# Moving the logit group, the Q/K stage and the small norm operations in a two-layer transformer kernel

## The chip, the cores and the metric

The kernel runs on one core of one Trainium2 chip. Its time is the device time of one execution in microseconds (us), as a median over executions. Two kernels are compared by a ratio: the mean time of one kernel's fast runs over the mean of the other's fast runs of the same rounds. It is therefore not quite the ratio of the medians that are quoted.

Engine names in the profile: PE is TensorE (matmul), PEld its weight load, DVE VectorE, ACT ScalarE, POOL GpSimd, and SPq the queue of the sync engine (SyncE), which issues nearly all DMAs of this program in program order.

## The reference

Two pairs of layers, with the same weights in both pairs. S = 2048 tokens, D = 1024, F = 3584, 32 heads of 32 channels, bf16.

```python
x = A_x
for _ in range(2):                                   # written out in the original
    x = x + _A_ref(_layernorm(x), A_wqkv, A_wo)      # attention over 8 keys, at distances 0, 2, ..., 14
    x = x + _B_ref(_layernorm(x), B_W_gate, B_W_up, B_W_down)
return x

# _A_ref: qkv = x @ wqkv; logits[s, w] = q[s] . k[s - 2w] * Dh**-0.5; softmax over w;
#         o[s] = sum_w attn[s, w] * v[s - 2w]; return o @ wo
# _B_ref: gate = x @ W_gate; h = relu(gate) * (x @ W_up); return h @ W_down
```

## The kernel before

The work is cut into 8 blocks of 512 tokens (blocks 0 to 3 are the first pair of layers, 4 to 7 the second). A loop runs over the blocks n. One pass does four things on TensorE:

1. the gated unit of block n: 28 pairs of gate and up groups, 448 matmuls of 128x512;
2. the output projection of the attention of block n+1 (64 matmuls), after which the second norm of block n+1 can begin;
3. Q/K of block n+2 (128 matmuls) and, from block 4 on, V (64 matmuls);
4. the down projection of block n, in two halves of 112 matmuls. Each half reads four weight slabs of up to 1 MB, `wd_0_0` to `wd_0_3` and `wd_1_0` to `wd_1_3`.

Meanwhile VectorE forms the products q·k for 8 offsets and sums them over the channel groups; one small matmul group `L` (the logit group, eight matmuls) reduces them over the channels; then come the softmax and the weighting of V on VectorE. The normed block goes to the next matmuls through a transposing DMA of 1 MB (called the copy below). A scheduler orders the instructions of each engine from the order in which they are emitted, the waits, and its own estimate of durations. It also orders the DMAs of SyncE.

The weight slabs come through a ring of five buffers, loaded by SyncE. Cuts are marked `...`.

```python
wring = ctx.enter_context(tc.tile_pool(name="wring", bufs=5))
...
def load_slab(src_ap, name):
    ...
    nc.sync.dma_start(tv, src_ap)
...
def ln_steps(n, which, early=False):       # which: "a" = norm ahead of attention, "b" = ahead of the gated unit
    ...
    def small():                           # once for the four tiles of a block
        st = hold["st"]
        ...
        nc.vector.tensor_scalar(mean[:], st[:, 0, :], 1.0 / D, None, op0=ALU.mult)
        nc.vector.tensor_tensor(nvar[:], st[:, 0, :], mean[:], op=ALU.mult)
        nc.vector.tensor_tensor(nvar[:], nvar[:], st[:, 1, :], op=ALU.subtract)
        nc.vector.tensor_scalar(vpe[:], nvar[:], -1.0 / D, EPS, op0=ALU.mult, op1=ALU.add)
        nc.gpsimd.tensor_tensor(rstd[:], vpe[:], neg_half[:], op=ALU.pow)
        nc.vector.scalar_tensor_tensor(nb[:], mean[:], -1.0, rstd[:], op0=ALU.mult, op1=ALU.mult)
        ...
    def apply(t):
        def f():
            ...
            nc.scalar.activation(hold["xn"][:, t, :], xt[:], ACT.Identity, scale=hold["rstd"][:, t:t + 1],
                                 bias=hold["nb"][:, t:t + 1])
            if t == TPB - 1:
                ...
                nc.sync.dma_start_transpose(hold["xnT"][:].rearrange("p t k n -> p (t k) n"),
                                            hold["xn"][:].rearrange("p t d -> p (t d)"))
        return f
...
    for n in range(NN):
        gu, hold = gu_steps(n, ln_b[n])
        spread(ev, gu, at, 2 * GRP)                      # ev: (time, step) pairs, emitted in order of time
        ...
        if n + 1 < NN:
            spread(ev, wo_steps(n + 1), at, 2 * GRP)     # output projection
            ln2(n + 1, at + 4.5)                         # second norm and its copy
            at += 2 * GRP * TPB
        if n + 2 < NN:
            spread(ev, qk_steps(n + 2, ln_a[n + 2]), at, 2 * GRP)
            sums, red = prod_sum_steps(n + 2)
            spread(ev, sums, at + 3.6, 4.4)
            ev.append((at + 75.5, red))                  # logit group
            ev.append((at + 76.0, lambda n=n: softmax(n + 2)))
            ...
        down = down_steps(n, hold)
        spread(ev, down, at, 4 * GRP)
```

## Time and profile before

The median was 1696.95 us over 3 runs (1695.44 to 1698.25). The profiled execution has a span of 1696.5 us and a mean granted TensorE clock of 0.988 of full speed.

| What | us |
|---|---|
| span | 1696.5 |
| PE busy | 1637.1 (97%) |
| 8 matmuls of 128x512, start to start, undisturbed | 1.727 |
| first gated unit waits for its transposed norm | 11.8 |
| logit groups of blocks 2 to 7 wait for the last sum | 2.9 to 4.9 each, 23.1 in all |

TensorE bounds the kernel, so what counts is where TensorE stands still. This is the line of busy times on the page of the kernel before (busy us, share of the span, instructions):

```profile
PE 1637.1 (97%) x7576; PEld 781.0 (46%) x7576; DVE 1064.2 (63%) x973; ACT 482.8 (28%) x777; POOL 172.5 (10%) x168
```

These are PE's waits in the kernel before. A line gives the tile and line of code that waited, what released it, the sum in us, the number of waits, and the longest.

```profile
PE acc_g L448 <- DMA xnT_b_1286<-xn_b_1168: 11.8, 1, 11.8
...
PE L_2670 L298 <- DVE s_2235 L340: 4.9, 1, 4.9
PE L_9605 L298 <- DVE s_9153 L340: 4.1, 1, 4.1
PE L_6767 L298 <- DVE s_6315 L340: 3.8, 1, 3.8
PE L_4001 L298 <- DVE s_3566 L340: 3.8, 1, 3.8
PE L_5349 L298 <- DVE s_4897 L340: 3.6, 1, 3.6
PE L_8184 L298 <- DVE s_7732 L340: 2.9, 1, 2.9
```

`acc_g` is the first gate group; the `L_` lines are the six logit groups. Most of these holes cost more than their length, as the timeline of PE in the kernel before shows around the first of them (start, length, engine, line, operation, out<-in, count, and in brackets the idle time and its releaser):

```profile
359.36 0.61 PE L298 MATMUL L_2670<-s_2235,sel 128*32 128x512 bf16 x4 [4.89 <-DVE s_2235 L340]
359.90 1.03 PE L474 MATMUL dacc_2550<-wd_1_3_2690,hT_1339 128*128 128x512 bf16 x2
360.73 1.69 PE L474 MATMUL dacc_2551<-wd_1_3_2690,hT_1339 128*128 128x512 bf16 x4
```

Two matmuls, from 359.90 to 360.73, take 0.83 us, that is 0.42 us each, where 0.216 is the undisturbed pace. The Trainium skill ("TensorE: Matmul & The Clock Gate", Part 1: The HAM clock gate) explains such a pace: after an idle window of about 3.4 us the array runs at half clock until it has been busy for about as long.

### The profile page before, as it was taken

Reading aid. Unit: us, or ns where it says so; the run is one execution under the profiler, and the core shown is the slowest. Engines: PE = TensorE matmul, PEld = TensorE weight load, DVE = VectorE, ACT = ScalarE, POOL = GpSimd, SP = SyncE. Lnnn points to the kernel's source line nnn. Section 1 sums busy time; section 2 is a strip of 40 time slices with the busy share of each in tenths; the row PEclk is TensorE's granted clock in tenths of the full one; section 3 lists DMA queues with packets and bytes.
Section 4 is the critical chain, followed back from the end, with each engine's and each line's share of the span. In section 5 each row is a group of like instructions: output and inputs, shape, how many; then the busy total and the mean of one; then the engine's idle time right before and its main releaser. Section 6 shows DMA issues by size and latency. Waiting matters only on the chain.

```text
span 1696.5 us, 18303 instructions
## 1 busy us (share of the span) xinstructions
PE 1637.1 (97%) x7576; PEld 781.0 (46%) x7576; DVE 1064.2 (63%) x973; ACT 482.8 (28%) x777; POOL 172.5 (10%) x168
## 2 busy tenths in 40 slices
PE   7997999989999999999999999999999999999999
PEld 3543445534454444534455344554445434444444
DVE  2699794997279943998149971499615995121111
ACT  7834414023240324222142221422215101130110
POOL 1210002300050001200013000230004100000000
PEclk9998999999999999999999999999999999999999
DMA  8576758546755384766547666476854946465442
GB/s 288 88 193 146 192 172 210 184 139 185 222 143 181 125 224 149 192 158 200 173 158 209 158 186 189 146 203 169 229 171 125 244 156 198 149 191 181 149 152 72
DMA packets 370692, 296.78 MB, mean 175 GB/s; under 512 B 142257, under 2 KB 351153, under 8 KB 369585
## 3 DMA queue, kind: packets, MB, share of 16 engines
q1 hardware_dynamic: 370320, 295.10, 61.0%
q8 instruction: 59, 0.97, 0.2%
q10 hardware_dynamic: 288, 0.52, 0.1%
q14 instruction: 25, 0.20, 0.0%
HBM read 256.77 MB, written 21.00 MB: 164 GB/s over the span
## 4 chain that ended last, share of the span: by engine, by line
PE 64%; DVE 25%; ACT 4%; DMA 3%; issue 2%; POOL 2%; DVEq 0%; SPq 0%; POOLq 0%; ACTq 0%
PE acc_g L448 23%; PE acc_u L448 23%; PE acc_wo L423 7%; DVE ac_0_2236 L340 1%; DVE ac_1_5145 L340 1%; DVE ac_1_3813 L340 1%; DVE ac_1_2482 L340 1%; DVE ac_1_9401 L340 1%; DVE ac_1_7980 L340 1%; DVE ac_1_6563 L340 1%; PE acc_q L273 1%; PE acc_k L273 1%; POOL rstd L165 1%; PE acc_v L242 1%; DVE ac_0_3567 L340 1%
## 5 line engine op out<-in xcount | busy, mean ns | idle before, releaser
L453 ACT ACTIVATE r<-acc_g 128x512 bf16<-128x512 f32 x224 | 133.2, 595 | 637.2 <-PE acc_g L448 628.5
L165 POOL TENSOR_TENSOR rstd<-vpe,neg_half 128x4 f32<-128x4 f32 x17 | 22.5, 1326 | 1181.5 <-DVE vpe L163 1181.5
L357 ACT ACTIVATE d<-d 128x1024 f32<-128x1024 f32 x8 | 8.5, 1057 | 258.3 <-DVE d L356 258.3
L454 DVE TENSOR_TENSOR hT_10755<-acc_u,r 128x512 bf16<-128x512 f32 x28 | 19.4, 692 | 77.4 <-PE acc_u L448 77.4
L454 DVE TENSOR_TENSOR hT_9720<-acc_u,r 128x512 bf16<-128x512 f32 x28 | 19.4, 692 | 53.0 <-PE acc_u L448 53.0
L454 DVE TENSOR_TENSOR hT_6878<-acc_u,r 128x512 bf16<-128x512 f32 x28 | 19.3, 691 | 52.8 <-PE acc_u L448 52.8
L454 DVE TENSOR_TENSOR hT_5461<-acc_u,r 128x512 bf16<-128x512 f32 x28 | 19.3, 690 | 52.5 <-PE acc_u L448 52.5
L454 DVE TENSOR_TENSOR hT_8299<-acc_u,r 128x512 bf16<-128x512 f32 x28 | 19.3, 691 | 51.2 <-PE acc_u L448 51.2
L454 DVE TENSOR_TENSOR hT_4043<-acc_u,r 128x512 bf16<-128x512 f32 x28 | 19.3, 690 | 39.7 <-PE acc_u L448 39.7
L454 DVE TENSOR_TENSOR hT_2712<-acc_u,r 128x512 bf16<-128x512 f32 x28 | 19.3, 688 | 38.9 <-PE acc_u L448 38.9
L474 PEld LDWEIGHTS <-hT_4043 128*128 128x128 bf16 x224 | 22.5, 101 | 28.6 <-issue 3.9
L474 PEld LDWEIGHTS <-hT_5461 128*128 128x128 bf16 x224 | 22.5, 101 | 28.5 <-issue 3.7
L474 PEld LDWEIGHTS <-hT_2712 128*128 128x128 bf16 x224 | 22.4, 100 | 28.5 <-issue 3.7
L474 PEld LDWEIGHTS <-hT_8299 128*128 128x128 bf16 x224 | 22.2, 99 | 27.7 <-issue 2.4
L474 PEld LDWEIGHTS <-hT_1339 128*128 128x128 bf16 x224 | 22.0, 99 | 27.4 <-issue 2.0
L474 PEld LDWEIGHTS <-hT_10755 128*128 128x128 bf16 x224 | 21.9, 98 | 26.4
L474 PEld LDWEIGHTS <-hT_9720 128*128 128x128 bf16 x224 | 21.9, 98 | 26.4
L474 PEld LDWEIGHTS <-hT_6878 128*128 128x128 bf16 x224 | 21.8, 98 | 26.4 <-issue 0.2
L454 DVE TENSOR_TENSOR hT_1339<-acc_u,r 128x512 bf16<-128x512 f32 x28 | 19.3, 690 | 19.7 <-PE acc_u L448 16.3
L448 PE MATMUL acc_g<-xnT_b_1286,wg_0_1340 128*128 128x512 bf16 x32 | 9.2, 441 | 11.8 <-DMA xnT_b_1286<-xn_b_1168 11.8
L359 DVE TENSOR_REDUCE ssum<-d 128x128 f32<-128x1024 f32 x8 | 15.4, 1924 | 5.6 <-ACT d L357 5.6
L298 PEld LDWEIGHTS <-sel 128*32 128x32 bf16 x120 | 2.9, 95 | 34.4 <-issue 34.0
(1893 smaller groups left out, 3872.3 us busy)
## 6 DMA issues: line engine op xcount, KB each, us to landing
vhm_372<-v_d SPq DMA_DIRECT2D x4, 284.0 KB, 5.7
vhm_1298<-v_d SPq DMA_DIRECT2D x4, 284.0 KB, 8.9
vhm_2480<-v_d SPq DMA_DIRECT2D x4, 284.0 KB, 6.1
vhm_3811<-v_d SPq DMA_DIRECT2D x4, 284.0 KB, 9.1
vhm_5235<-v_d SPq DMA_DIRECT2D x4, 284.0 KB, 6.6
vhm_6653<-v_d SPq DMA_DIRECT2D x4, 284.0 KB, 6.4
vhm_8070<-v_d SPq DMA_DIRECT2D x4, 284.0 KB, 7.2
vhm_9491<-v_d SPq DMA_DIRECT2D x4, 284.0 KB, 6.0
```

Source lines behind the costliest of these rows:

```text
L165: nc.gpsimd.tensor_tensor(rstd[:], vpe[:], neg_half[:], op=ALU.pow)
L242: nc.tensor.matmul(acc[:], lhsT=sl[g][:, kc, col:col + P], rhs=ln["xnT"][:, :, kc, :], start=(kc == 0), stop=(kc == KC - 1))
L273: nc.tensor.matmul(acc[:], lhsT=w, rhs=ln["xnT"][:, :, kc, :], start=(kc == 0), stop=(kc == KC - 1))
L298: nc.tensor.matmul(st["L"][32 * tq:32 * tq + 32, WH * wh:WH * (wh + 1), :], lhsT=sel[:], rhs=prod[:, WH * wh:WH * (wh + 1), tq * P:(tq + 1 ...
L340: nc.vector.tensor_tensor(o, ac[:], t[:], op=ALU.add)
L357: nc.scalar.activation(d[:], d[:], ACT.Exp, scale=scale)
L359: nc.vector.tensor_reduce(ssum[:], d[:].rearrange("p w t -> p t w"), axis=AX.X, op=ALU.add)
L423: nc.tensor.matmul(acc[:], lhsT=st["oT"][:, c, t, :], rhs=sl[half][:, c, :], start=(c == 0), stop=(c == KC - 1))
L448: nc.tensor.matmul(acc[:], lhsT=hold[nm][:, kc, jl * P:(jl + 1) * P], rhs=ln["xnT"][:, :, kc, :], start=(kc == 0), stop=(kc == KC - 1))
L453: nc.scalar.activation(r[:], acc[:], ACT.Relu)
L454: nc.vector.tensor_tensor(hold["hT"][:, j, :], accs["u"][:], r[:], op=ALU.mult)
L474: nc.tensor.matmul(ac[t], lhsT=hT[:, j, t * P:(t + 1) * P], rhs=wsl[:, jl, :], start=(j == 0), stop=(j == FC - 1))
```

## The change

Its intent was to take out the holes listed above:

1. The logit group of block n+2 and its softmax go out of the down projection into the next gated unit, behind the first pair of gate and up groups.
2. Q/K (and V) of block n+2 go ahead of the output projection of block n+1, so that VectorE's products and sums begin earlier. The two halves of the projection are run one after the other, and the Q and K groups get a new order among themselves.
3. The order of TensorE's groups is fixed by explicit edges, so that the scheduler cannot move them. One more edge puts each load of V (`vhm`) behind the slab load that was emitted last, and the opening ahead of the loop is timed anew; the cut below doesn't show these.
4. The small norm operations leave VectorE's queue: five ScalarE operations of 128x1 per tile, and one GpSimd power per tile in place of one per block. The second norm of block 0 is transposed tile by tile.

The core of the diff:

```diff
+    @contextmanager
+    def pe_group():
+        if tail_pe[0] is None:
+            yield
+        else:
+            with tc.issue_after(tail_pe[0]):
+                yield
...
-        def small():
-            st = hold["st"]
...                                        # the batch on VectorE shown above
+                nc.scalar.activation(nm2, sx, ACT.Square, scale=1.0 / D)
+                nc.scalar.activation(nm2, nm2, ACT.Identity, scale=-1.0, bias=eps_col[:])
+                nc.scalar.activation(vpe, sq, ACT.Identity, scale=1.0 / D, bias=nm2)
+                nc.gpsimd.tensor_tensor(rstd, vpe, neg_half[:, 0:1], op=ALU.pow)
+                nc.scalar.activation(mr, sx, ACT.Copy, scale=-1.0 / D)
+                nc.scalar.activation(nb, mr, ACT.Identity, scale=rstd)
...
+                if which == "b" and n == 0:
+                    nc.sync.dma_start_transpose(hold["xnT"][:, t, :, :], xn)
+                elif t == TPB - 1:
                     nc.sync.dma_start_transpose(hold["xnT"][:].rearrange("p t k n -> p (t k) n"),
                                                 hold["xn"][:].rearrange("p t d -> p (t d)"))
...
+        elif n + 1 < NN:
+            ev.append((at + 0.1, reds_n[n + 1]))
+            ev.append((at + 0.2, lambda n=n: softmax(n + 1)))
...
-        if n + 1 < NN:
-            spread(ev, wo_steps(n + 1), at, 2 * GRP)
-            ln2(n + 1, at + 4.5)
-            at += 2 * GRP * TPB
         if n + 2 < NN:
-            spread(ev, qk_steps(n + 2, ln_a[n + 2]), at, 2 * GRP)
+            spread(ev, qk_steps(n + 2, ln_a[n + 2]), at, GRP)
             sums, red = prod_sum_steps(n + 2)
-            spread(ev, sums, at + 3.6, 4.4)
-            ev.append((at + 75.5, red))
-            ev.append((at + 76.0, lambda n=n: softmax(n + 2)))
+            reds_n[n + 2] = red
+            spread(ev, sums, at + GRP * (K_STEP[0] + 1.0), 4.4)
...
+        if n + 1 < NN:
+            spread(ev, wo_steps(n + 1), at, 2 * GRP)
+            ln2(n + 1, [at + GRP * TPB + GRP * (t + 1) + 0.1 for t in range(TPB)])
+            at += 2 * GRP * TPB
```

## The prediction

> **What bounds it now.** TensorE. The page shows PE 97% busy; in the timeline 8 matmuls of 128x512 start every 1.727 us, so the 7424 of them cost 1603 us. With 15.2 us before, 15 logit groups of 0.55 and 4.3 us after, the floor is about 1631 us. The span is 1696.5: some 60 us are holes in TensorE's stream.
>
> **The holes (PE's waits and timeline).**
> - Logit groups of blocks 2 to 7 stand inside the down projection and wait for the last DVE sum: 4.9, 3.8, 3.6, 3.8, 2.9, 4.1 us. Afterwards matmuls start every 0.42 us for 2 to 4 us; together about 34 us.
> - First gated unit: 11.8 us for the transposed norm of block 0, plus 1.6 us of slow clock. Its chain: small norm operations on DVE queued behind 2.3 us sums (145.4 to 155.8), applies 4.6 us, one 1 MB transpose 6.8 us.
> - First output projection: 2.1 us for its DMA, 1.7 us slow.
> - Q/K of block 0: 3 to 4 us of waits for products; ACT is busy 35 of 40 us there.
> - K weights: 0.3 to 1.6 us per block, 3 us in all.
>
> The Trainium skill ("TensorE: Matmul & The Clock Gate", Part 1) says an idle window of about 3.4 us drops the array to half clock; this trace agrees (0.42 us per matmul after the 11.8 us hole).
>
> **What the change does.** No matmul is added or removed. The logit group goes behind the first gate/up pair of the next gated unit; Q/K moves ahead of the output projection. The sums take 67.6 us of DVE (30 operations of 2.26 us). They now have Q/K (27.6) + V (13.8) + output projection (13.8) + down (48.4) + 3.5 us, less 8 us until the first K: 99 us, without V (blocks 2, 3) 85. DVE needs 76 to 78 with its evictions of 0.64 us. So all six waits should go. The first gated unit's norm leaves the DVE queue and is transposed per tile: its input should come about when V of block 3 ends, so the 12 us go. Cost: five 128x1 ACT operations per norm tile, estimated 0.1-0.2 us each (the 128x1 accumulator read lasts 0.19), 5-10 us in the opening, where ACT is full; and ACT now waits in order for POOL's power (1.0 to 3.0 us). So the opening gains little, and the first projection still waits for its DMA.
>
> **Sum.** 1697 - 33 (logit groups) - 14 (first gated unit) - 3 (K weights) = 1647 us. All of it lies on the critical path (TensorE).
>
> **Predicted: 1647 us, range 1637 to 1664.** Faster by over 2%: 0.90; within 2%: 0.09; slower: 0.01.
>
> **What would show it.** Logit groups of blocks 2-7 waiting under 0.5 us, sums ending some 10 us before them; granted clock near 1.00 from the first gated unit on, which starts at 152-157 us instead of 167; first projection still waiting 2-4 us; ACT over 85% busy from 30 to 70 us.
>
> **What would make it wrong.** The down projection's second half needs banks whose evictions now stand behind the sums in DVE's order (from block 4 on, with under 2 us of slack by my estimate): holes of 1-3 us per block, with slow clock after them. ACT delaying Q/K in the opening by 5 us or more. POOL, slowed by DVE, holding ACT and the gate evictions. The second K weight slab landing late.

## More of the kernel before

One more view matters, and the prediction did not weigh it: the timeline of SyncE's queue in the kernel before, where block 1 is normed (start us, length of the issue, queue, line, kind of DMA, out<-in).

```profile
291.56 4.91 SPq L177 DMA_TRANSPOSE xnT_b_2241<-xn_b_2117  x1
...
305.28 0.40 SPq L134 DMA_DIRECT2D wd_0_1_2446<-in_B_W_down_dram  x1
...
307.87 1.06 SPq L134 DMA_DIRECT2D wd_1_0_2553<-in_B_W_down_dram  x1
```

The copy of block 1's second norm is issued at 291.56, some 16 us ahead of the slab `wd_1_0`. The output projection's matmuls end at 280.0, so the norm takes about 11.5 us from there to the copy.

## The result, and the profile after

The kernel after took 1721.7 us (median of 4 runs, 1720.78 to 1723.74); the kernel before took 1696.24 (median of 4 in the same comparison). The ratio is 1.015 (95% interval 1.0132 to 1.0168): the change made the kernel 1.5% slower. The predicted time, 1647, and its whole range lie below what was measured. The profiled span is 1719.2 us at a mean granted clock of 0.978.

The busy line of the page of the kernel after, with columns as before:

```profile
PE 1637.0 (95%) x7576; PEld 781.2 (45%) x7576; DVE 1047.8 (61%) x888; ACT 534.5 (31%) x1117; POOL 273.7 (16%) x220
```

TensorE has the same work to the last instruction, in a longer span: the loss is idle time. These are PE's waits in the kernel after:

```profile
PE dacc_2642 L104 <- DMA wd_1_0_2646<-in_B_W_down_dram: 12.2, 1, 12.2
PE dacc_3999 L104 <- DMA wd_1_0_4003<-in_B_W_down_dram: 12.2, 1, 12.2
...
PE dacc_9780 L104 <- DMA wd_1_0_9784<-in_B_W_down_dram: 8.1, 1, 8.1
PE dacc_5446 L104 <- DMA wd_1_0_5450<-in_B_W_down_dram: 8.0, 1, 8.0
PE dacc_6890 L104 <- DMA wd_1_0_6894<-in_B_W_down_dram: 7.9, 1, 7.9
PE dacc_8333 L104 <- DMA wd_1_0_8337<-in_B_W_down_dram: 7.8, 1, 7.8
PE acc_g L104 <- DMA xnT_b_1207<-xn_b_1206: 5.1, 1, 5.1
```

The six logit groups are gone from the list, as intended. In their place stand six waits for the slab `wd_1_0`, one in each down projection of blocks 0 to 5: 56.2 us in all. The list says "DMA". It does not say why the DMA came late. The timeline of SyncE's queue in the kernel after says it, in the pass that corresponds to the one shown before:

```profile
294.23 0.37 SPq L151 DMA_DIRECT2D wd_0_3_2613<-in_B_W_down_dram  x1
294.64 1.86 SPq L399 DMA_DIRECT2D vhm_2567<-v_d  x1
326.87 4.90 SPq L186 DMA_TRANSPOSE xnT_b_2429<-xn_b_2428  x1
331.87 0.52 SPq L151 DMA_DIRECT2D wd_1_0_2646<-in_B_W_down_dram  x1
```

Nothing is issued for 30 us, from 296.5 to 326.87. Then comes the copy, and only behind it the slab, although nothing in the slab's load depends on the copy. The queue is in order, and it stood waiting for the norm. The table of busy times in that stretch shows the DMA engines were not the limit (the window, then us, busy time and count of PE, PEld, DVE, ACT and POOL, granted clock, DMA share, GB/s):

```profile
290.00:331.90 41.90, 35.28 (x164) 15.79 (x162) 41.76 (x29) 16.85 (x40) 17.38 (x6) 0.95 0.46 92
```

The DMA engines were busy 46% of it and moved 92 GB/s, against 173 on average over this span. VectorE, on the other hand, was busy throughout: 41.76 of 41.90 us.

What it costs is in the timeline of PE in the kernel after:

```profile
324.25 1.03 PE L104 MATMUL dacc_2482<-wd_0_3_2613,hT_1392 128*128 128x512 bf16 x4
337.51 3.60 PE L104 MATMUL dacc_2642<-wd_1_0_2646,hT_1392 128*128 128x512 bf16 x8 [12.23 <-DMA wd_1_0_2646<-in_B_W_down_dram]
340.89 2.03 PE L104 MATMUL dacc_2643<-wd_1_0_2646,hT_1392 128*128 128x512 bf16 x8
...
367.03 0.61 PE L104 MATMUL L_2801<-s_2208,sel 128*32 128x512 bf16 x8
```

The first 8 matmuls behind the hole take 3.38 us, 0.42 each: half pace again, 1.65 us lost beyond the 12.2. In the hole that goes with the norm of block 3 (8.0 us, in the down projection of block 2) it is 1.66 us in the first 8 and 0.51 in the next 8. An estimate for six holes: 56.2 us and some 2 us each, 68 us. The last line above answers to the first of the `L_2670` lines before: the logit group starts with no wait.

Why was the norm so late? The projection's matmuls end at 300.9, and the copy is issued 26 us later (11.5 before). Two parts make it up. First, the projection's evictions now stand in VectorE's order among products and sums of 2.3 us each, because Q/K comes first: the last eviction ends at 307.0, 6.0 us behind the matmuls (0.9 before). Secondly, from there to the copy it takes 19.9 us (10.6 before), and GpSimd shows most of the reason. The timeline of POOL in the kernel after, the four powers of block 1's second norm:

```profile
301.97 2.01 POOL L173 TENSOR_TENSOR st_b_2427<-st_b_2427,neg_half 128x1 f32<-128x1 f32 x1 [10.74 <-ACT st_b_2427 L172]
309.19 7.00 POOL L173 TENSOR_TENSOR st_b_2427<-st_b_2427,neg_half 128x1 f32<-128x1 f32 x1 [5.21 <-ACT st_b_2427 L172]
...
318.12 2.60 POOL L173 TENSOR_TENSOR st_b_2427<-st_b_2427,neg_half 128x1 f32<-128x1 f32 x1
322.62 2.62 POOL L173 TENSOR_TENSOR st_b_2427<-st_b_2427,neg_half 128x1 f32<-128x1 f32 x1 [1.91 <-ACT st_b_2427 L172]
```

The same line of code, taken over the whole program, gives the duration with VectorE at rest, in block 7 (op, count, ns min/median/max, first and last start), and who waited for it (us, times):

```profile
L173 POOL TENSOR_TENSOR st_b_10661<-st_b_10661,neg_half x4: 548/550/551, 1522.9 to 1532.4; 128x1 f32<-128x1 f32 x4
...
  ACT st_b_2427 L175: 11.3, 4
```

A power of 128x1 takes 0.55 us at rest and 2.0 to 7.0 us next to the products and sums. The Trainium skill ("GPSIMD Engine Reference", Specifications) states that GpSimd shares its SBUF interfaces with VectorE and contends with VectorE instructions that have two SBUF inputs. The products and sums are such instructions, and this trace agrees. ScalarE, in order, waited 11.3 us for these four powers.

### The profile page after: what moved, and what is told of

Read it like the earlier page. It is cut to its first block, busy times and chain, and to the rows that moved or that the text cites. A ratio compares the mean times of both kernels' runs of the same rounds, so it can differ in the third digit from the quotient of the medians.

```text
span 1719.2 us, 18662 instructions
## 1 busy us (share of the span) xinstructions
PE 1637.0 (95%) x7576; PEld 781.2 (45%) x7576; DVE 1047.8 (61%) x888; ACT 534.5 (31%) x1117; POOL 273.7 (16%) x220
## 4 chain that ended last, share of the span: by engine, by line
PE 65%; DVE 11%; ACT 5%; POOL 4%; issue 3%; DMA 2%; SPq 2%; DVEq 0%; ACTq 0%; POOLq 0%
PE acc_g L104 23%; PE acc_u L104 22%; PE acc_q L104 3%; SPq L186 2%; PE acc_k L104 1%; POOL st_b_3784 L173 1%; PE acc_wo L104 1%; DVE ac_0_7810 L363 1%; DVE ac_0_9257 L363 1%; DVE ac_0_6367 L363 1%; POOL st_b_5235 L173 0%; POOL st_b_6679 L173 0%; POOL st_b_8122 L173 0%; PE dacc_5446 L104 0%; PE dacc_6890 L104 0%
## 5 line engine op out<-in xcount | busy, mean ns | idle before, releaser
L104 PEld LDWEIGHTS <-hT_7019 128*128 128x128 bf16 x224 | 22.5, 101 | 36.4 <-DMA wd_1_0_8337<-in_B_W_down_dram 8.3
L104 PEld LDWEIGHTS <-hT_5575 128*128 128x128 bf16 x224 | 22.5, 101 | 36.3 <-DMA wd_1_0_6894<-in_B_W_down_dram 8.3
L173 POOL TENSOR_TENSOR st_b_10661<-st_b_10661,neg_half 128x1 f32<-128x1 f32 x4 | 2.2, 550 | 159.2 <-ACT st_b_10661 L172 159.2
L173 POOL TENSOR_TENSOR st_a_8704<-st_a_8704,neg_half 128x1 f32<-128x1 f32 x4 | 6.7, 1680 | 73.3 <-ACT st_a_8704 L172 73.3
L173 POOL TENSOR_TENSOR st_a_5814<-st_a_5814,neg_half 128x1 f32<-128x1 f32 x4 | 6.7, 1682 | 73.2 <-ACT st_a_5814 L172 73.2
L173 POOL TENSOR_TENSOR st_a_7257<-st_a_7257,neg_half 128x1 f32<-128x1 f32 x4 | 6.7, 1680 | 73.2 <-ACT st_a_7257 L172 73.2
```

The source lines that it names most:

```text
L104: tail_pe[0] = nc.tensor.matmul(*args, **kwargs).ins
L173: nc.gpsimd.tensor_tensor(rstd, vpe, neg_half[:, 0:1], op=ALU.pow)
```

## The experiments

Theory (call it the queue theory): the whole loss comes from the place of the copy in SyncE's queue, ahead of `wd_1_0`, together with a norm that is late. Rivals: the lateness of the norm by itself; GpSimd's slow powers; the order of Q/K and projection; the edges; the norm operations on ScalarE. The edge on the V loads has no run of its own, but e1, e2 and e10 keep it and have no slab wait. In each of the short diffs below the kernel is compared with the kernel after, unless said otherwise.

The results in one table. The ratio is to the kernel before in the same rounds; "slab waits" is the sum of TensorE's waits for `wd` in the profiled run.

| Run | median us | ratio (95%) | slab waits us |
|---|---|---|---|
| e1, copy behind `wd_1_2` | 1650.79 | 0.9731 (0.9715 to 0.9748) | none |
| e2, copy from ScalarE's queue | 1651.67 | 0.9734 (0.9719 to 0.9748) | none |
| e3, no GpSimd power (wrong result) | 1668.14 | 0.9832 (0.9818 to 0.9847) | 13.7 |
| e4, before + logit group moved | 1662.09 | 0.9795 (0.9781 to 0.981) | none |
| e5, projection first again | 1678.93 | 0.9892 (0.9877 to 0.9907) | none |
| e6, one power per block | 1697.14 | 1.0006 (0.9987 to 1.0024) | 31.1 |
| e7, e1 + e6 | 1652.85 | 0.9739 (0.9725 to 0.9754) | none |
| e8, no edges on TensorE | 1721.34 | 1.0144 (1.0129 to 1.0159) | 56.4 |
| e10, small norm operations back on VectorE | 1653.67 | 0.9744 (0.973 to 0.9757) | none |
| e11, e10 + copy ahead of the slab | 1727.99 | 1.0182 (1.0168 to 1.0196) | 63.0 |
| e9, e1 + sums held back in the opening | 1648.04 | 0.971 (0.9697 to 0.9723) | none |

The medians of the kernel before lay between 1696.89 and 1697.34 us in the three sets of runs (e1 to e4; e5 to e8; e9 to e11). All results but that of e3 were correct.

### e1: the copy of the second norm behind the third slab of the down projection's second half

```diff
-                elif t == TPB - 1:
-                    nc.sync.dma_start_transpose(...)
+                elif t == TPB - 1 and which == "a":
+                    xpose()
...
+        def xpose_late():
+            with tc.issue_after(tail_sp[0]):       # behind the last slab load emitted so far: wd_1_2
+                xpose()
...
         spread(ev, down, at, 4 * GRP)
+        if n + 1 < NN:
+            ev.append((at + 4 * GRP * 6 + 0.5, ln_b[n + 1]["late"]))
```

> The changed kernel with one edit: the transposed copy of the second norm (blocks 1 to 7) is issued behind the down projection's slab loads instead of ahead of four of them. Theory Q (the copy, whose input is ready only at 326.9 us in block 1, stands at the head of SyncE's DMA queue and holds the slab that TensorE needs): the six holes of 12.2, 12.2, 8.0, 7.9, 7.8, 8.1 us and the slow clock after them (about 2.5 us each) go, about 71 us, so 1645 to 1660 us, with the copy landing some 10 us before the next gated unit. Theory N (the second norm is simply too late for what follows): the holes move to the first gate matmuls of the next gated unit, over 5 us each, and the time stays above 1690. Theory F (the fixed TensorE order forbids other work from filling in): no change, 1715 to 1725, since the order stays.

Measured: 1650.79 us. The norm is as late as ever: this is SyncE's queue in e1, where `wd` stands for any of the down slabs.

```profile
315.24 0.37 SPq L151 DMA_DIRECT2D wd<-in_B_W_down_dram  x1
327.16 4.87 SPq L190 DMA_TRANSPOSE xnT_b<-xn_b  x1
332.13 0.53 SPq L151 DMA_DIRECT2D wd<-in_B_W_down_dram  x1
```

The copy is issued at 327.16 (326.87 in the kernel after), but three slabs of the second half are already on their way. The edge was meant to put the copy behind all of them; the last one, `wd_1_3`, still comes behind it, in every block. TensorE needs that slab last (in the kernel after its matmuls start 22.5 us behind those of `wd_1_0`), and no slab wait is left. The next gate group starts at 349.58 without a wait. The span falls from 1719.2 to 1649.0 us, 70.2 us, beside the estimate of 68 above, and the granted clock rises to 0.999. A late norm costs nothing here; a late norm ahead of a load that TensorE needs at once does.

### e2: the copy issued from ScalarE's queue

```diff
-                    nc.sync.dma_start_transpose(...)
+                    (nc.scalar if which == "b" else nc.sync).dma_start_transpose(...)
```

> The changed kernel with the same copy at the same place in the program, but issued from ScalarE's DMA queue (all second norms), so that SyncE's queue holds no wait for the norm. Theory Q: 1645 to 1660 us, no wait for the down slabs above 1 us, although the norm itself is as late as before (copy issued at about 325 to 330 us in block 1). Theory N: as above, waits at the next gated unit, over 1690. Theory F: no change. A cost of about 5 us of ScalarE per block for issuing may show, off the critical path.

Measured: 1651.67 us, no slab waits. The edit moves the copies of blocks 1 to 7; block 0's, tile by tile, stay on SyncE's queue. The timeline of ACT in e2 shows the copy behind the last apply, as late as before, and again without harm:

```profile
326.78 1.24 ACT L182 ACTIVATE xn_b<-x,st_b 128x1024 bf16<-128x1024 bf16 x1
328.05 5.95 ACTq L186 DMA_TRANSPOSE xnT_b<-xn_b  x1
```

This says the same as e1 with a different edit: it is SyncE's queue that was held. The Trainium skill ("DMA: Bandwidth & Descriptors", Anatomy of one DMA — SWDGE (gpsimd) path) states that a DMA's semaphore wait happens on the issuing sequencer before dispatch. That section is written for DMAs issued by GpSimd; the timelines agree for SyncE, which in the kernel after issued nothing for 30 us. The same page (Silent corruption: two transposing streams in flight at once) warns that transposes issued from two engines may not overlap in time. In e2 the two kinds of copy lie in different stages, and its result was correct; e1 does not raise the question.

### e3: no power on GpSimd in the second norms of blocks 1 to 7 (wrong result)

```diff
-                nc.gpsimd.tensor_tensor(rstd, vpe, neg_half[:, 0:1], op=ALU.pow)
+                if which == "b" and n > 0:
+                    nc.scalar.activation(rstd, vpe, ACT.Identity)
+                else:
+                    nc.gpsimd.tensor_tensor(rstd, vpe, neg_half[:, 0:1], op=ALU.pow)
```

> The changed kernel, with GpSimd's power of the second norm (blocks 1 to 7) replaced by a copy on ScalarE of the same size; the result is wrong on purpose. The queue order stays as in the changed kernel. Theory P (the copy is late because four powers per block, 0.55 us each when VectorE rests, took 1.3 to 7.0 us beside the sums, and ScalarE waited 11.3 us for them in blocks 1 and 2 and 5.2 us in 3 to 6): the copy is issued 10 us or more earlier in block 1 and about 5 us earlier in blocks 3 to 6; holes under 2 us in blocks 1 and 2, 2 to 4 us in the others; 1655 to 1680 us. Rival V (the copy is late because the projection's evictions stand behind the sums on VectorE, whatever GpSimd does): the holes stay at 7 us or more each, over 1700 us.

Measured: 1668.14 us; relative error 0.031. The copy of block 1 is issued at 316.50, 10.4 us earlier than in the kernel after, and the slab waits shrink from 56.2 to 13.7 us, none longer than 2.9. (In e3 the projection itself ends 0.8 us later, so the copy is 11.1 us earlier as counted from there.) So in the changed kernel GpSimd's slow powers make most of the lateness that hurts, but not all of it.

### e4: the kernel before, with only the logit group moved (against the kernel before)

```diff
-            ev.append((at + 75.5, red))
-            ev.append((at + 76.0, lambda n=n: softmax(n + 2)))
+            reds_n[n + 2] = red
...
-                spread(ev, pv_steps(n + 1), at + 4.0, 9.0)
+                ev.append((at + 0.1, reds_n[n + 1]))
+                ev.append((at + 0.2, lambda n=n: softmax(n + 1)))
+                spread(ev, pv_steps(n + 1), at + 12.0, 6.5)
```

> The kernel before with one part of the change alone: the logit group and softmax move to the next gated unit; projection still ahead of Q/K, norm operations on VectorE in a batch, no order edges. By my sum the six waits and their slow clock (about 34 us) go and nothing is put in their place: 1658 to 1672 us, waits of the logit groups under 1 us. If instead the group's place was not what cost the time, the time stays at 1690 or more.

Measured: 1662.09 us, 35.3 less than the 1697.34 of the kernel before beside it. No logit group of blocks 2 to 7 waits. This one move, a few lines, is worth what the prediction gave it (33), although the first gated unit now waits 14.1 us instead of 11.8.

### e5: the output projection ahead of Q/K again

```diff
         at += 2 * GRP * FC
+        if n + 1 < NN:
+            spread(ev, wo_steps(n + 1), at, 2 * GRP)
+            ln2(...)
+            at += 2 * GRP * TPB
         if n + 2 < NN:
             ...                                    # Q/K and V
-        if n + 1 < NN:
-            ...                                    # the same lines
```

> The changed kernel with one part undone: the output projection again ahead of Q/K (group still in the next gated unit, norm on ScalarE, edges kept). Theory V+P (the norm is late because its evictions and powers now run beside the sums on VectorE; that follows from moving Q/K ahead): the norm of blocks 1 to 6 ends 12 to 16 us after the projection instead of 21 to 27, before the sums are under way, no wait for down slabs, 1645 to 1662 us; the logit groups of blocks 2 and 3 may wait up to 3 us, as the sums have only 72 us there. Rival S (the small norm operations on ScalarE and GpSimd are late by themselves, wherever the projection stands): the norm is as late as before and down slabs still wait several us, over 1680 us.

Measured: 1678.93 us, which misses the expected time. The slab waits go, as expected: with 128 more matmuls between the projection and the second half of the down projection, the norm has time. Block 1's copy is issued 14.1 us behind the projection's end, within the expected 12 to 16, so rival S falls: where the projection stands matters. But two other waits appear: block 1's projection waits 11.2 us for its attention output, and the logit groups of blocks 2 and 3 wait 8.6 us together. These waits don't show that Q/K has to be early, because e5 keeps other parts of the change: the weighting of V for block 1 is emitted 58 us into the gated unit instead of 40, and in the new order of the Q and K groups the first sum of block 2 starts 13.0 us behind the projection. In e4, which has the projection first with the old order, it starts 8.8 us behind it, and no logit group of blocks 2 to 7 waits.

### e6: the power once per block

```diff
-                nc.gpsimd.tensor_tensor(rstd, vpe, neg_half[:, 0:1], op=ALU.pow)
                 nc.scalar.activation(mr, sx, ACT.Copy, scale=-1.0 / D)
-                nc.scalar.activation(nb, mr, ACT.Identity, scale=rstd)
+                if which == "a":
+                    ...                            # as before
+                elif t == TPB - 1:
+                    nc.gpsimd.tensor_tensor(hold["st"][:, :, 4], hold["st"][:, :, 3], neg_half[:], op=ALU.pow)
+                    for i in range(TPB):
+                        nc.scalar.activation(hold["st"][:, i, 6:7], hold["st"][:, i, 5:6], ACT.Identity,
+                                             scale=hold["st"][:, i, 4:5])
...
-            ev.append((a + 4.0, apply[t]))
+            ev.append((ats[-1] + 4.0 + 0.1 * t, apply[t]))
```

> The changed kernel with one power of 128x4 per second norm in place of four of 128x1 (result right; queue order kept). Theory P: ScalarE waits once instead of four times; the copy is issued some 5 to 9 us earlier in blocks 1 and 2, 6 us in 3 to 6; holes shrink to 5 to 9 us in blocks 1 and 2 and 0 to 3 us in the others; 1675 to 1695 us. If the powers are not the cause: as the changed kernel, 1715 to 1725.

Measured: 1697.14 us, just above the range expected. The slab waits fall to 31.1 us, but the first gated unit now waits 9.7 us instead of 5.1: block 0 wants its tiles one by one. Four powers in place of one, with the applies that are emitted between them, cost some 25 us of slab waits; e6 changes both at once.

### e7: e1 and e6 together

The diff is that of e1 and that of e6.

> A candidate for the best: the copy issued behind the down slabs (as in the run with the late copy) and one power per second norm. No holes after the first gated unit; that unit's wait of 5.2 us shrinks to 2 to 4 us, as its last apply no longer follows four powers: 1645 to 1651 us, at or slightly below the late copy alone (1650.8).

Measured: 1652.85 us, just above the range expected and not better than e1. With the copy out of the way of the slabs, the powers of blocks 1 to 7 cause no slab wait, four or one; the wait of the first gated unit, 10.0 us, was expected to shrink and did not.

### e8: no edges on TensorE's order

```diff
     def pe_group():
-        if tail_pe[0] is None:
+        if True:
             yield
```

> The changed kernel without the order edges between matmul groups. The built order of TensorE is the same but for four matmuls in Q/K of block 0. Theory F (the edges cost the time): under 1700 us. All others: 1715 to 1726 us, the same six waits for down slabs.

Measured: 1721.34 us and 56.4 us of slab waits: the same as the kernel after. The edges are innocent. (As the order was built almost the same without them, e8 does not test that order.)

### e10: the small norm operations of blocks 1 to 7 back on VectorE, as one batch

```diff
+                if which == "b" and n > 0:
+                    if t == TPB - 1:
+                        ...                        # the four operations, the power and nb, as in the kernel before
+                    return
                 nc.scalar.activation(nm2, sx, ACT.Square, scale=1.0 / D)
...
-            ev.append((a + 4.0, apply[t]))
+            ev.append((a + 4.0 if n == 0 else ats[-1] + 4.0 + 0.1 * t, apply[t]))
```

> The changed kernel with one part undone: the second norm's small operations (blocks 1 to 7) again on VectorE in a batch with one power. In the built program VectorE's small operations stand between sums, and the tile scheduler puts the transposed copy two slab loads later in SyncE's queue than in the changed kernel (behind the second slab of the down projection's second half instead of ahead of the first). Theory Q: no wait for down slabs, 1648 to 1665 us, although the copy is issued no earlier than in the changed kernel (26.6 us after the projection's end in block 1; here 24 to 32 us): it is the place in the queue that cost the time, and ScalarE's shorter small operations cost time only as they moved that place. Rival (ScalarE and GpSimd made the norm late, VectorE would be quicker): the copy is issued 5 us or more earlier than in the changed kernel.

Measured: 1653.67 us without any slab wait, but not because the norm came earlier. SyncE's queue in e10:

```profile
307.56 0.37 SPq L151 DMA_DIRECT2D wd<-in_B_W_down_dram  x1
...
325.83 4.88 SPq L196 DMA_TRANSPOSE xnT_b<-xn_b  x1
330.82 1.20 SPq L151 DMA_DIRECT2D wd<-in_B_W_down_dram  x2
```

The copy of block 1 goes out at 325.83, only 1 us earlier than in the kernel after, and in blocks 3 to 6 the time from last eviction to copy is even longer (19.6 us, against 17.8). What differs is the place: in the order that the scheduler built, the copy now stands behind `wd_1_0` and `wd_1_1`. In the kernel after it stands ahead of `wd_1_0`. The scheduler places the copy by its own estimate of when the norm is ready, and with the small operations on ScalarE it puts it two slabs earlier. That this estimate is the reason is argued from the two built orders; the estimate itself appears in no trace.

### e11: e10, with the copy forced to the place that it has in the kernel after

```diff
+                if half == 1 and s8 == 0 and n + 2 < NN:
+                    with tc.issue_after(ln_b[n + 1]["copy"]):
+                        wsl = load_slab(src, f"wd_{n}_{half}_{s8}")
+                else:
+                    wsl = load_slab(src, f"wd_{n}_{half}_{s8}")
```

> The same kernel, with one order edge per block that puts the copy back ahead of the down projection's fifth slab load, where the changed kernel has it. Theory Q: the six holes come back, as large as the copy is late: copy issue plus 4.9 us of issuing plus about 5.6 us of load, less the time of the first half; 10 to 16 us each in blocks 1 and 2, 8 to 14 in the others, 1710 to 1750 us. If the place in the queue does not matter: as the run without the edge, within 3 us.

Measured: 1727.99 us. This is SyncE's queue in e11, in the same stretch, and below it PE's slab waits:

```profile
326.54 4.90 SPq L196 DMA_TRANSPOSE xnT_b<-xn_b  x1
331.54 1.19 SPq L151 DMA_DIRECT2D wd<-in_B_W_down_dram  x2
```

```profile
PE dacc L104 <- DMA wd<-in_B_W_down_dram: 63.0, 6, 11.9
```

e10 and e11 do the same work with the same norm, whose copy is issued 0.7 us apart. One edge per block, which moves two slab loads from one side of the copy to the other, makes 74 us (1727.99 − 1653.67). That settles the cause: the place of the copy decides whether its lateness costs anything.

### e9: e1, with part of VectorE's sums held back in the opening

```diff
...                                                # the edit of e1
-    spread(ev, sums1, at + 46.0, 4.4)
+    spread(ev, sums1[:6], at + 46.0, 4.4)
...
+    def hold_sums():                               # an instruction that reads the last power of block 0's norm
...
+        gate["i"] = nc.vector.tensor_copy(gate["t"][:], ln_b[0]["st"][:, TPB - 1, 4:5]).ins
...
+    spread(ev, [after_gate(f) for f in sums1[6:]], at + 2 * GRP * TPB + 0.3, 4.2)
```

> A candidate for the best: the late copy, and VectorE holds the remaining sums of block 1 until block 0's second norm has its last power (a 128x1 copy of it is placed ahead of them). Theory P (a power is slow only beside VectorE's sums of two operands in SBUF): the last powers of block 0's second norm take about 0.55 us instead of 1.2 to 2.2, its last apply ends 4 to 7 us earlier (157.6 before), the first gated unit's wait of 5.2 us shrinks under 1.5 us; 1643 to 1648 us. The logit group of block 1 should still not wait. If the powers stay slow with VectorE resting, theory P falls.

This one looks at what is left: the first gated unit's wait, and the contention on GpSimd by itself. The powers of block 0's second norm, POOL's timeline first in the kernel after, then in e9:

```profile
144.49 2.24 POOL L173 TENSOR_TENSOR st_b_1205<-st_b_1205,neg_half 128x1 f32<-128x1 f32 x1 [6.68 <-ACT st_b_1205 L172]
147.32 1.83 POOL L173 TENSOR_TENSOR st_b_1205<-st_b_1205,neg_half 128x1 f32<-128x1 f32 x1 [0.59 <-ACT st_b_1205 L172]
```

```profile
144.11 0.55 POOL L173 TENSOR_TENSOR st_b<-st_b,neg_half 128x1 f32<-128x1 f32 x1 [6.68 <-ACT st_b L172]
147.02 0.55 POOL L173 TENSOR_TENSOR st_b<-st_b,neg_half 128x1 f32<-128x1 f32 x1 [2.36 <-ACT st_b L172]
```

With VectorE's sums held back (VectorE is idle from 141.6 to 152.2), the same powers take 0.55 us each: the slowing comes from VectorE's work. The first gated unit starts at 157.87 (160.84 in e1), but TensorE still waits 4.1 us there, for nothing that the profile shows, where under 1.5 was expected. The likely cause, argued from the timelines and not tested: the last tile's copy is issued only at 154.18, behind its apply on ScalarE, 3.7 us before the unit starts. The median is 1648.04 us, the lowest of all: 2.9% less than the kernel before, and less than the kernel after. Its margin over e1 (1650.79, in another set of runs) is not resolved by the ratios, whose intervals just overlap. The traces put it all in the opening: from the start of the first gated unit on, both take 1488 us.

## Why the prediction was wrong

The sum was "1697 - 33 (logit groups) - 14 (first gated unit) - 3 (K weights) = 1647 us". Point by point:

- **TensorE is the bound, about 1631 us of floor.** Right: PE's busy time is 1637.0 after and 1637.1 before, and with the new hole removed e1 runs at 1650.79.
- **Logit groups, −33.** Right. Their waits are gone in the kernel after, and e4, which moves only the group, the softmax and the weighting of V behind it, gains 35.3 us. As foretold, block 2's group does not wait: its sums end at 343.1 us, 23.9 ahead of the group at 367.0. The holes add to that lead; in e1, without them, the sums end at 343.4, 9.7 ahead of the group at 353.1, as foretold (some 10).
- **First gated unit, −14.** The mechanism was right, its size was not. The gated unit starts at 160.71 instead of 167.37, a gain of 6.7 us; 152 to 157 had been expected. The norm did leave VectorE's queue, but its powers still contend with VectorE's sums, and 5.1 us of wait remain. In e9, without that contention, the unit starts 3.0 us earlier than in e1, so it explains a part only.
- **K weights, −3.** Right: no wait for `wk` is left in the list.
- **First projection still waits 2 to 4 us.** Right: 2.4 us. ScalarE over 85% busy from 30 to 70 us: right, 38.13 of 40 us (95%); but as it was 37.29 before the change, this shows little.
- **Granted clock near 1.00.** Wrong in the kernel after (0.978), because of the six new holes; 0.999 in e1.
- **The step that failed is an omission from the sum.** It counted the holes that the change removes, and gave the second norm of block 0 a line. It priced the move of the small norm operations in the opening only ("5-10 us in the opening"), and gave no line to the second norms of blocks 1 to 6, which the change also touches: their small operations move, their evictions now stand behind the sums, and there are fewer matmuls between the projection and the second half of the down projection. Their copies sit in SyncE's in-order queue, ahead of `wd_1_0`. In the runs that term was +70 us (56.2 us of waits and the slow pace after each), and it ate the gain of some 46.
- **The risks that were named.** "POOL, slowed by DVE, holding ACT" did happen (11.3 us of ScalarE's waits in block 1), but its way to TensorE, through a DMA queue, was not seen. ScalarE's wait alone is harmless, as e1 shows. The feared waits of the second half for its evictions did not appear among the large ones: the second half did stall, but for its weight slab.

The slack, though not the lateness, could have been estimated before running: the trace before has the issue of such a copy (4.91 us) and the loads of its slabs. With the numbers of the kernel after: in the new order 112 matmuls (24.2 us at 1.727 us for 8) lie between the end of the projection and the second half. The slab takes 5.6 us from issue to the first matmul (331.87 to 337.51), and the copy's issue 5.0 us. To be in time, the copy must go out within 24.2 − 5.6 − 5.0 = 13.6 us of the projection's end. In the kernel before the norm takes 11.5 us with its operations in one batch on an almost idle VectorE; the change put the norm next to the busiest stretch of VectorE. It took 26, so the wait should be about 12.4 us: 12.2 was measured. In e3 the copy is issued at 316.50, 10.4 us earlier, which leaves some 2 us of wait for block 1: 1.3 was measured there.

Without the jam the kernel takes what was predicted, within 4 us: 1650.79 in e1. That is closer than the terms of the sum deserve: the first gated unit gave some 7 us less than its 14, and the logit groups, by e4, some 2 us more than their 33. (e9, with 1648.04, has an edit that the prediction did not cover.)

## What to carry to other kernels

A queue that issues DMAs in order is a resource of its own: for every DMA that waits for computed data, look at what stands behind it in the same queue and when TensorE needs that, and put such a copy behind the loads that must not wait, or on another queue. When a change shifts work between engines, cost the late finishers too, by the slack that the new order leaves them, and not only the waits that the profile of before lists. A small operation on GpSimd must be costed at the length that it has next to the VectorE work that it will now run beside.

## What the Trainium skill lacked or had wrong

- "DMA: Bandwidth & Descriptors" (Issuing engines are not separate DMA queues) says that issuing from several engines only saves the sequencer's time to initiate the DMA, usually small beside the transfer. Here it saved far more: issuing the second norm's copy from ScalarE's queue took the kernel from 1721.7 to 1651.67 us (e2), because independent loads no longer stood behind a DMA that waited for its input. The page states that the wait happens on the issuing sequencer, but does not draw this conclusion. The nearest advice is that of "Perfetto Trace Analysis" (DMA Optimizations), to give inputs and outputs separate issuing engines.
- "GPSIMD Engine Reference" (Specifications) names the contention with VectorE instructions that have two SBUF inputs, but gives no size there; the skill's page "SBUF — State Buffer" (Who interferes with whom) goes further into it, but not to a small power beside a stream of sums. Here a power of 128x1 took 0.55 us with VectorE at rest and 1.3 to 7.0 us in the second norms of blocks 1 to 6 beside products and sums (times on POOL are rough in this profiler, but the order of size is plain); held apart from them it took 0.55 again (e9).
- "DMA: Bandwidth & Descriptors" gives the time for which a transpose within SBUF occupies its issuing sequencer only as a count of cycles for 8,192 tiles, in a comparison of an older generation with a newer one. Here one of 1 MB took 4.9 us of SyncE's queue and 5.95 us of ScalarE's (e2, block 1).
